# Output product of a fused attention and FFN kernel: the sums and low parts of each chunk from the fifth on moved from GpSimd to VectorE

## The chip, the cores and the metric

One NeuronCore of one Trainium2 chip runs the whole program. The metric is the device time of one execution in microseconds, as the median of three runs. Engines are written as in the profile: PE is TensorE (PEld its weight loads), DVE is VectorE, ACT is ScalarE, POOL is GpSimd, SP is SyncE, which here only issues DMAs.

## The reference

```python
def reference(q, k, v, moe_w1, moe_w2, moe_w3, moe_w_out, moe2_w_in, moe2_w_out):
    attn = attention(q, k, v)            # 4 x 8 heads, 576 positions, causal window of 64, head_dim 64
    x = attn.transpose(0, 2, 1, 3).reshape(2304, 512)
    h = np.maximum(np.maximum(x @ moe_w1, x @ moe_w2), x @ moe_w3)   # 512 -> 768
    x = h @ moe_w_out                                                # 768 -> 512
    h = x @ moe2_w_in                                                # 512 -> 2048
    g = np.where(h >= 1, h, np.where(h <= -1, 0.0, (h + 1) ** 2 / 4))
    return g @ moe2_w_out                                            # 2048 -> 512, the output product
```

## The kernel before

Attention and the first FFN come first, then the product with `moe2_w_in`, and last the output product `g @ moe2_w_out`, which is the only part that the change touches. Each float32 operand is used as two numbers of fewer bits, a high part and a low part (what is left of the value after the high part), and a product takes three passes: high with high, high with low, low with high (`PASSES`).

The output product is written as a Strassen-like scheme with seven products in place of eight. It needs seven blocks for each operand: four quarters and three sums of quarters, one quarter being replaced by a difference. `sums` lists the four additions and subtractions that make them:

```python
        return (
            (x[4], x[2], x[3], ALU.add), (x[2], x[0], x[2], ALU.subtract),
            (x[5], x[4], x[0], ALU.subtract), (x[6], x[1], x[5], ALU.subtract),
        )
```

The 2304 tokens are cut into nine blocks of 256, and the 2048 inner dimensions into four pieces, so that there are 36 chunks (`NCH`), numbered k, with `k % 4` the piece and `k // 4` the token block. The fifth chunk is k = 4. For a chunk, `g_load` brings four quarters from DRAM (`g_scratch` in the profile) into a staging tile `plain`, of which there are three. `g_steps` lists eight steps on it: the four sums (`combine`, line 503 in the profile, L503), then for the first four of the seven blocks a copy to the high part on ACT (`act_copy`, L113, 128x1024) and the low part (`low`, L116, 128x1024), then the same two for the last three blocks (128x768). The high and low parts lie in one of four regions, used in turn (`gc[k % 4]`): two in the tile `side`, two in `arena`. The PE then runs 42 matmuls for the chunk (`d_mm`, L940): two halves r, seven products, three passes. The weights of the product stand in `side`, `arena` and `left`. After every fourth chunk `d_out` (L952 on DVE, one copy on ACT) puts the seven products of a token block together from PSUM, in tiles `evt` and `ut`, and sends the result out.

The order on PE, ACT and DVE is the order in which the steps were put into a list by hand-written times (`put2`, `staged`); `chained` holds these three engines to it. The steps of chunk k stand 2.4 chunks ahead of its matmuls, one after the other, with the parts of `d_out` of the token block before in between. POOL's and SP's order follows the program too. A copy to a region waits until PE is through with the chunk that used it four chunks earlier, and a load waits until the low parts of the chunk that used the staging tile three chunks earlier are made.

In the kernel before, from k = 4 on the second sum (i = 1) is made on POOL, and from k = 5 on the low part of the last three blocks too; the rest is on DVE.

Of the kernel before, what the change touches and what calls it, by code (L numbers as in the profile page):

```python
# [68 lines left out]
def kernel(ctx, tc, q, k, v, w1, w2, w3, wo1, wi2, wo2, out, x2d, td, gd):  # L69
# [12 lines left out]
    nc = tc.nc  # L82
# [378 lines left out]
    RA = {1: 0, 2: 1, 7: 2, 4: 3, 5: 4, 6: 5, 3: 6}  # L461
# [126 lines left out]
    for h in range(2):  # L588
        r = slice(h * BL, h * BL + BL)
# [312 lines left out]
    def quarter(x, q):  # L902
        i, j = divmod(q, 2)
        return x[:, 2 * j:2 * j + 2, i * P:(i + 1) * P] if q < 4 else x[:, q].rearrange("p (r t) -> p r t", r=2)
# [5 lines left out]
    def g_steps(k):  # L910
        c, x = gc[k % 4], plain["g", k]
        steps = [
            (combine, (nc.gpsimd if k == 1 or (k > 3 and i == 1) else nc.vector, [quarter(x, q) for q in range(7)], RA, i))
            for i in range(4)
        ]
        for r in (slice(0, 4), slice(4, 7)):
            hi, lo = (o[:, r] for o in c.hl)
            eng = nc.gpsimd if (k < 1 or k > 4) and r.stop == 7 else nc.vector
            steps += [(act_copy, (hi, x[:, r])), (low, (eng, lo, x[:, r], hi))]
        return steps  # L920

# [54 lines left out]
    for k in range(NCH):  # L976
        if k < 4:
            put2((26.4, 27.2, 30.9, 31.9)[k], g_load, k)
            steps_at(((27.05, 27.06, 27.07, 28.06, 29.01, 29.05, 29.57, 29.58),
                      (28.1, 28.11, 28.12, 28.13, 29.9, 30.05, 30.58, 31.05),  # L980
                      (32.02, 32.03, 32.04, 32.05, 32.31, 32.41, 32.33, 32.43),
                      (32.70, 32.71, 32.72, 32.73, 32.74, 32.76, 32.75, 32.77))[k], g_steps, k)
        else:
            put2(end + CU * (k - 3.4 - (0.4 if k > 4 else 0.0)), g_load, k)
            staged(put2, end + CU * (k - 2.4), 0.06, 8, g_steps, k)
# [30 lines left out]
```

## Time and profile before

| what | value |
|---|---|
| median of three runs | 783.17 us (783.16 to 783.36) |
| profiled execution | 782.92 us |
| its span, first to last instruction | 781.1 us |
| mean granted TensorE clock | 0.987 of full speed |
| busy: PE, DVE, ACT, POOL | 750.4, 511.4, 424.2, 379.8 us |

The busy times are sums over the span, and a busy PE is not PE at its peak: matmuls are pipelined and the ends of the records are modelled, so that how fast PE gets on is better read from the starts of equal pieces of work. The output product fills the last quarter of the span.

### The profile page before, as it was taken

What the parts mean: (1) busy time and instruction counts of PE and PEld (TensorE: products, weight loads), DVE (VectorE), ACT (ScalarE), POOL (GpSimd) and SP (SyncE); (2) the same over time, 40 slices, a digit from 0 to 9 for tenths busy, and PEclk for the clock granted to TensorE, in tenths of its full rate; (3) what the DMA queues carried; (4) which work ended last, traced back from release to release, by engine and by line L of the source; (5) the groups of instructions that cost most, each with busy time, mean ns of one, the idle gap of its engine ahead of it and who ended that gap; (6) DMA issues with size and microseconds to landing.
All of it is one profiled execution on the core that took longest, in us unless ns stands there. A gap on an engine that the chain in (4) does not pass through costs nothing.

```text
span 781.1 us, 17634 instructions
## 1 busy us (share of the span) xinstructions
PE 750.4 (96%) x6824; PEld 728.1 (93%) x6824; DVE 511.4 (65%) x1074; ACT 424.2 (54%) x855; POOL 379.8 (49%) x409
## 2 busy tenths in 40 slices
PE   4798999999999999999999999999999999999997
PEld 3598999999999999999999999999999999999997
DVE  4777334455634454632656687767878899999996
ACT  5897645455464454552448766767685333333332
POOL 1767422544544363553448433731377445555552
PEclk9599999999999999999999999999999999999999
DMA  9999641447767549543445543554556344344341
GB/s 269 264 259 262 162 110 47 144 152 184 227 136 251 202 110 253 197 169 119 135 137 188 200 152 122 178 200 173 195 186 202 123 135 122 122 137 134 113 132 55
DMA packets 158244, 130.00 MB, mean 166 GB/s; under 512 B 94928, under 2 KB 139984, under 8 KB 158160
## 3 DMA queue, kind: packets, MB, share of 16 engines
q1 hardware_dynamic: 135552, 86.13, 39.8%
q10 hardware_dynamic: 19024, 28.06, 9.8%
q0 software_dynamic: 3584, 14.68, 4.8%
q8 instruction: 53, 0.87, 0.5%
q14 instruction: 31, 0.25, 0.1%
HBM read 85.85 MB, written 42.99 MB: 165 GB/s over the span
## 4 chain that ended last, share of the span: by engine, by line
PE 56%; DVE 15%; issue 8%; ACT 7%; POOL 4%; SPq 3%; DMA 3%; ACTq 1%; POOLq 0%; DVEq 0%
PE ps L428 22%; PE ps L450 8%; DVE plain L503 7%; PE cc L747 5%; PE ce L747 5%; PE ca L747 5%; SPq L267 3%; PE cb L747 2%; DVE arena L116 2%; DVE side L116 2%; POOL plain L503 2%; ACT arena L113 2%; PE pps L381 1%; PE sps L339 1%; PE ops L402 1%
## 5 line engine op out<-in xcount | busy, mean ns | idle before, releaser
L428 PE MATMUL ps<-xt,arena 128*128 128x256 f32 x1944 | 237.6, 282 | 6.0 <-ACT xt L113 2.9
L428 PEld LDWEIGHTS ps<-xt,arena 128*128 128x128 f32 x1944 | 231.7, 190 | 8.8 <-ACT xt L113 3.1
L503 DVE TENSOR_TENSOR plain<-plain 128x256 f32<-128x256 f32 (+1 forms) x140 | 128.2, 919 | 3.0 <-DMA plain<-g_scratch 1.3
L116 POOL TENSOR_TENSOR arena<-plain,arena 128x256 fp32r<-128x256 f32 (+2 forms) x70 | 76.8, 1125 | 75.3 <-ACT arena L113 67.2
L437 DVE TENSOR_TENSOR ht<-ps,ht 128x256 f32<-128x256 f32 x108 | 45.3, 420 | 94.8 <-PE ps L428 50.8
L113 ACT ACTIVATE arena<-plain 128x1024 fp32r<-128x1024 f32 (+1 forms) x64 | 61.2, 959 | 66.4 <-POOL plain L503 53.9
L116 POOL TENSOR_TENSOR side<-plain,side 128x768 fp32r<-128x768 f32 (+2 forms) x40 | 56.1, 1422 | 69.8 <-ACT side L113 69.8
L450 PE MATMUL ps<-h,arena 128*128 128x256 f32 x648 | 79.6, 281 | 0.8 <-ACT ht L113 0.8
L450 PEld LDWEIGHTS ps<-h,arena 128*128 128x128 f32 x648 | 76.9, 188 | 2.0 <-issue 1.0
L116 POOL TENSOR_TENSOR h<-ht,h 128x256 fp32r<-128x256 f32 x54 | 44.4, 823 | 68.7 <-ACT h L113 68.4
L113 ACT ACTIVATE side<-plain 128x1024 fp32r<-128x1024 f32 (+3 forms) x48 | 45.4, 965 | 58.2 <-POOL plain L503 44.5
L113 ACT ACTIVATE h<-ht 128x256 fp32r<-128x256 f32 x54 | 22.6, 418 | 81.6 <-DVE ht L437 81.5
L372 POOL TENSOR_TENSOR sm<-sm,rs 128x512 f32<-128x512 f32 (+1 forms) x36 | 35.8, 995 | 59.6 <-DVE rs L371 44.8
L362 ACT ACTIVATE sm<-sm,nm 128x128 f32<-128x128 f32 (+1 forms) x144 | 55.2, 389 | 5.0 <-DVE nm L350 4.2
L210 DVE CUSTOM_DVE_ANT_0 wt<-wst,wt 128x1024 uint16<-128x1024 uint16 (+1 forms) x44 | 45.7, 1046 | 2.4 <-ACT wst L113 1.1
L835 ACT ACTIVATE ut<-ut 128x288 f32<-128x288 f32 x64 | 43.9, 686 | 2.0
L116 DVE TENSOR_TENSOR arena<-plain,arena 128x1024 fp32r<-128x1024 f32 (+3 forms) x28 | 34.8, 1248 | 15.1 <-ACT arena L113 15.1
L503 POOL TENSOR_TENSOR plain<-plain 128x256 f32<-128x256 f32 x36 | 30.8, 855 | 20.5 <-POOL arena L116 6.2
L113 ACT ACTIVATE x2s<-ps 128x256 f32<-128x256 f32 x36 | 13.8, 383 | 49.4 <-PE ps L450 36.4
L116 DVE TENSOR_TENSOR side<-plain,side 128x1024 fp32r<-128x1024 f32 (+3 forms) x25 | 31.0, 1243 | 13.9 <-ACT side L113 13.8
L116 POOL TENSOR_TENSOR arena<-wt,arena 128x512 fp32r<-128x512 f32 x24 | 35.3, 1498 | 9.3 <-ACT arena L113 9.1
L116 DVE TENSOR_TENSOR xt<-ops,xt 128x512 fp32r<-128x512 f32 (+1 forms) x22 | 13.0, 591 | 39.2 <-ACT xt L113 39.2
(144 smaller groups left out, 1622.2 us busy)
## 6 DMA issues: line engine op xcount, KB each, us to landing
g_scratch<-ut ACTq DMA_DIRECT2D x64, 288.0 KB, 2.5
plain<-g_scratch SPq DMA_DIRECT2D x36, 512.0 KB, 3.8
plain<-t_scratch SPq DMA_DIRECT2D x16, 896.0 KB, 4.7
wst<-in_moe_w_out SPq DMA_DIRECT2D x22, 512.0 KB, 4.7
wst<-in_moe_w SPq DMA_DIRECT2D x18, 512.0 KB, 6.5
wst<-in_moe_w_in SPq DMA_DIRECT2D x16, 512.0 KB, 5.0
t_scratch<-wt POOLq DMA_DIRECT2D x16, 512.0 KB, 3.4
vr<-in_v SPq DMA_DIRECT2D x24, 256.0 KB, 4.7
```

The lines of the kernel that those rows point to most:

```text
L113: nc.scalar.activation(dst, src, AF.Copy, scale=scale)
L116: eng.tensor_tensor(dst, a, b, op=ALU.subtract)
L210: nc.vector.tensor_tensor(t[:, x], t[:, x], st[:, x, 0], op=ALU.add)
L267: nc.sync.dma_start(t[32 * a:32 * a + 32, p], src[b1, 2 * p + a // 2, i1 * BL:(i1 + CH) * BL, 32 * (a % 2):32 * (a % 2) + 32] .rearrange(" ...
L362: nc.scalar.activation(sm[:, p, 0:W], sm[:, p, 0:W], AF.Exp, bias=d["nm"][:, p:p + 1], scale=-1.0, accum_out=ss[:, p:p + 1])
L372: nc.gpsimd.tensor_tensor(sm[:, :, 0:W], sm[:, :, 0:W], rs.unsqueeze(2).to_broadcast([P, NP, W]), op=ALU.mult)
L428: nc.tensor.matmul(ps[:, 0:n], w_col((w, f), wl, kt), xt[:, xl, kt, 0:n], start=(x == 0), stop=(x == len(passes) - 1))
L437: nc.vector.tensor_tensor(t[:, 0:n], ps[:, 0:n], part[j, f][:, 0:n], op=ALU.max)
L450: nc.tensor.matmul(ps[:, 0:n], w_col((3, f), wl, dt), hts[j, f][:, xl, 0:n], start=(x == 0), stop=(x == len(passes) - 1))
L503: eng.tensor_tensor(o, a, b, op=op)
L747: nc.tensor.matmul(o, wt.of(m, wl)[:, kt * P:(kt + 1) * P], wx.of(m, xl)[:, kt], start=start and x == 0, stop=x == len(passes) - 1, skip_g ...
L835: nc.scalar.activation(o, o, AF.Square)
```

## The change

Both conditions that send work of the later chunks to GpSimd are taken away. From k = 4 on the second sum, and from k = 5 on the low part of the last three blocks, are issued on VectorE, in the place of the list where they stood. The condition for the first two chunks stays.

```diff
@@ def g_steps(k)
         c, x = gc[k % 4], plain["g", k]
         steps = [
-            (combine, (nc.gpsimd if k == 1 or (k > 3 and i == 1) else nc.vector, [quarter(x, q) for q in range(7)], RA, i))
+            (combine, (nc.gpsimd if k == 1 else nc.vector, [quarter(x, q) for q in range(7)], RA, i))
             for i in range(4)
         ]
         for r in (slice(0, 4), slice(4, 7)):
             hi, lo = (o[:, r] for o in c.hl)
-            eng = nc.gpsimd if (k < 1 or k > 4) and r.stop == 7 else nc.vector
+            eng = nc.gpsimd if k < 1 and r.stop == 7 else nc.vector
             steps += [(act_copy, (hi, x[:, r])), (low, (eng, lo, x[:, r], hi))]
         return steps
```

The order of DVE at chunks 4, 5 and 6, as a difference; `plain` with a number is the staging tile of one chunk (7856 is chunk 4's, 7893 chunk 5's, 7945 chunk 6's), and a low part is written to `side` or `arena`:

```order
-L503 TENSOR_TENSOR plain_7856<-plain_7856 128x256 x3
+L503 TENSOR_TENSOR plain_7856<-plain_7856 128x256
+L503 TENSOR_TENSOR plain_7856<-plain_7856 128x2x128
+L503 TENSOR_TENSOR plain_7856<-plain_7856 128x256 x2
 L116 TENSOR_TENSOR side_5246<-plain_7856,side_5246 128x1024
 L116 TENSOR_TENSOR side_5246<-plain_7856,side_5246 128x768
-L503 TENSOR_TENSOR plain_7893<-plain_7893 128x256 x3
+L503 TENSOR_TENSOR plain_7893<-plain_7893 128x256
+L503 TENSOR_TENSOR plain_7893<-plain_7893 128x2x128
+L503 TENSOR_TENSOR plain_7893<-plain_7893 128x256 x2
 L116 TENSOR_TENSOR side_5246<-plain_7893,side_5246 128x1024
+L116 TENSOR_TENSOR side_5246<-plain_7893,side_5246 128x768
```

The second sum (128x2x128) now stands between the first and the third, and from chunk 5 on the second low part follows the first one. Further on, DVE at chunk 8 (7997 is chunk 7's staging tile, 8050 chunk 8's) has two parts of `d_out` of the first token block between the sums:

```order
 L503 TENSOR_TENSOR plain_8050<-plain_8050 128x256
 L952 SCALAR_TENSOR_TENSOR ut_5818<-dx0_7802,evt_5817 128x256
+L503 TENSOR_TENSOR plain_8050<-plain_8050 128x2x128
 L503 TENSOR_TENSOR plain_8050<-plain_8050 128x256
 L952 SCALAR_TENSOR_TENSOR ut_5818<-dz0_7803,evt_5817 128x2x256
 L503 TENSOR_TENSOR plain_8050<-plain_8050 128x256
 L116 TENSOR_TENSOR side_5246<-plain_8050,side_5246 128x1024
+L116 TENSOR_TENSOR side_5246<-plain_8050,side_5246 128x768
```

Nothing else on DVE changed its place. POOL had these rows in the output product before, of which a piece over chunks 4 to 8 is shown, and has none of them now:

```order
L503 TENSOR_TENSOR plain<-plain 128x2x128 x2
L116 TENSOR_TENSOR side<-plain,side 128x768
L503 TENSOR_TENSOR plain<-plain 128x2x128
L116 TENSOR_TENSOR arena<-plain,arena 128x768
L503 TENSOR_TENSOR plain<-plain 128x2x128
L116 TENSOR_TENSOR arena<-plain,arena 128x768
L503 TENSOR_TENSOR plain<-plain 128x2x128
L116 TENSOR_TENSOR side<-plain,side 128x768
```

In all 32 sums and 31 low parts went from POOL to DVE. The rows of PE, ACT and SP are the same before and after.

## Rows read from the trace of the kernel before

**Rows 1.** The page, parts 1: span, busy time and instructions of each engine.

```profile
span 781.1 us, 17634 instructions
...
PE 750.4 (96%) x6824; PEld 728.1 (93%) x6824; DVE 511.4 (65%) x1074; ACT 424.2 (54%) x855; POOL 379.8 (49%) x409
```

**Rows 2.** PE in order of time, output product: start us, us, what.

```profile
593.74 0.87 PE L940 MATMUL dy<-arena,side 128*128 128x256 f32 x6
...
603.71 0.88 PE L940 MATMUL dy<-left,arena 128*128 128x256 f32 x6
...
608.66 0.88 PE L940 MATMUL dy<-side 128*128 128x256 f32 x6
...
613.64 0.86 PE L940 MATMUL dy<-arena,side 128*128 128x256 f32 x6
...
629.02 0.76 PE L940 MATMUL dy<-side 128*128 128x256 f32 x5
630.16 0.38 PE L940 MATMUL dy<-side 128*128 128x256 f32 x1 [0.38 <-POOL side L116]
...
634.65 0.86 PE L940 MATMUL dy<-arena,side 128*128 128x256 f32 x6
...
771.63 1.58 PE L940 MATMUL dy<-left,arena 128*128 128x256 f32 x12
```

**Rows 3.** Busy time by stretch, output product.

```profile
593.74:613.64 19.90, 19.90 (x171) 19.90 (x170) 17.57 (x19) 7.36 (x9) 11.09 (x10) 1.00 0.50 157
...
634.65:655.76 21.11, 20.58 (x171) 20.03 (x170) 19.31 (x22) 7.68 (x9) 11.06 (x9) 1.00 0.42 124
655.76:771.63 115.87, 113.20 (x926) 110.25 (x925) 105.99 (x118) 42.43 (x50) 60.37 (x45) 1.00 0.39 115
```

**Rows 4.** Waits from 600 us on: who, for whom, us in total, times, longest.

```profile
ACT arena L113 <- POOL plain L503: 53.9, 16, 3.6
...
POOL arena L116 <- ACT arena L113: 35.3, 16, 2.2
...
PE dy L940 <- POOL side L116: 2.4, 7, 0.4
```

**Rows 5.** POOL in order of time, one round of four chunks.

```profile
635.46 0.92 POOL L503 TENSOR_TENSOR plain<-plain 128x256 f32<-128x256 f32 x1 [0.41 <-POOL side L116]
638.56 1.89 POOL L116 TENSOR_TENSOR arena<-plain,arena 128x768 fp32r<-128x768 f32 x1 [2.18 <-ACT arena L113]
640.87 0.74 POOL L503 TENSOR_TENSOR plain<-plain 128x256 f32<-128x256 f32 x1 [0.42 <-POOL arena L116]
...
656.57 0.92 POOL L503 TENSOR_TENSOR plain<-plain 128x256 f32<-128x256 f32 x1 [0.41 <-POOL side L116]
```

**Rows 6.** DVE in order of time: without and beside POOL.

```profile
591.54 1.70 DVE L503 TENSOR_TENSOR plain<-plain 128x256 f32<-128x256 f32 x4 [1.31 <-DMA plain<-g_scratch]
...
601.74 2.08 DVE L116 TENSOR_TENSOR arena<-plain,arena 128x1024 fp32r<-128x1024 f32 x2
...
638.65 2.08 DVE L503 TENSOR_TENSOR plain<-plain 128x256 f32<-128x256 f32 x1
...
642.40 0.41 DVE L503 TENSOR_TENSOR plain<-plain 128x256 f32<-128x256 f32 x1
```

**Rows 7.** DVE groups by form, 613.64 to 771.63 us.

```profile
L503 DVE TENSOR_TENSOR plain<-plain 128x256 f32<-128x256 f32 x90 | 98.4, 1093 | 0.8
...
L952 DVE SCALAR_TENSOR_TENSOR evt<-dx,evt 128x512 f32<-128x512 f32 x8 | 5.4, 678 | 0.0
...
L952 DVE SCALAR_TENSOR_TENSOR evt<-dy,evt 128x256 f32<-128x256 f32 x8 | 3.3, 412 | 0.0
```

**Rows 8.** ACT in order of time: an issue and a copy.

```profile
626.57 0.65 ACTq L965 DMA_DIRECT2D out<-ut  x1
...
636.42 1.06 ACT L113 ACTIVATE arena<-plain 128x1024 fp32r<-128x1024 f32 x1 [3.59 <-POOL plain L503]
```

**Rows 9.** DMA issues, 590 to 640 us: size, us to landing.

```profile
plain<-g_scratch SPq DMA_DIRECT2D x10, 512.0 KB, 3.8
```

## Prediction

> **What bounds the kernel now.** I read the page first. PE is busy for 750.4 of 781.1 us [rows 1], so a change on DVE and POOL can matter only where PE waits. Records of PE end at modelled times, so I read its pace from the starts of chunks (PE in order of time). Chunks 1 to 4 of the output product start PE work at 593.74 and end where chunk 5 begins, at 613.64 [rows 2]: four chunks in 19.90 us, 4.98 each, with PE busy all the time at a granted clock of 1.00 [rows 3]. That is the pace of PE alone. From chunk 5 on it is not held: chunk 9 begins at 634.65 [rows 2], 21.01 us later, and the next round of four takes 21.11 us, still at 1.00 [rows 3]. So the loss is not the clock. Within chunk 8, which starts at 629.02, a matmul waits at 630.16 for a low part from POOL [rows 2]; the list of waits has this seven times for `side` alone [rows 4].
>
> What paces POOL? The waits name a ring: ACT waits 53.9 us for POOL's sums (into `arena`), POOL waits 35.3 us for ACT's copies there [rows 4]. POOL in order of time shows it: sum at 635.46, then 2.18 us idle for ACT, then the low part at 638.56 for 1.89 us, then the next sum at 640.87 [rows 5]. From 635.46 to 656.57 POOL makes four such turns in 21.11 us, exactly PE's round. POOL with ACT in series sets the pace, and PE follows.
>
> DVE looks nearly full at the same time: 19.31 of 21.11 us [rows 3]. But its sums take 1093 ns on average [rows 7], while the same form took 0.41 us at 642.40, when POOL ran nothing, and 2.08 us at 638.65, when POOL had started a low part 0.09 us earlier [rows 5, 6]. The 2.08 us end 0.28 us behind POOL's. Most of DVE's busy time is therefore waiting behind POOL.
>
> **The change part by part.** *POOL.* 32 sums and 31 low parts leave it. The ring ends, and from chunk 4 on nothing runs beside DVE.
>
> *DVE per chunk.* Without POOL four sums took 1.70 us, and the two low parts 2.08 us [rows 6]; both rows hold whole sequences, waits between dependent sums included. That is 3.78 us. Per four chunks: 4 x 3.78 = 15.12, and the five parts of `d_out`, three of 0.41 and two of 0.68 [rows 7], 2.59; together 17.7 us. ACT's first copy needs only the first two sums: it starts at about 0.85, takes 1.06 [rows 8], and with 0.03 us for each hand-over (an estimate; the copy at 636.42 starts 0.04 us behind POOL's sum [rows 5, 8]) ends at 1.97, when DVE has been through the sums for 0.27 us. So a chunk without `d_out` between its sums costs 0.85 + 0.03 + 1.06 + 0.03 + 2.08 = 4.05 us. In two chunks of four a part of 0.41 and one of 0.68 us stand among the sums, the wait vanishes, and the cost is 3.78 + 1.09 = 4.87 us. In one chunk a part of 0.41 us comes first and ACT then issues the output DMA, 0.65 us [rows 8], ahead of its copy, which starts 0.22 us late: 4.05 + 0.41 + 0.22 = 4.68. The round: 4.05 + 2 x 4.87 + 4.68 = 18.5 us on DVE, against 19.90 for PE. DVE is done 1.4 us earlier per round, and PE becomes the bound.
>
> *Start.* DVE has no stock at first. It ends chunk 3's low parts at 601.74 + 2.08 = 603.82 [rows 6]; 4.05 us later, at 607.87, chunk 4 is ready, and PE starts it at 608.66 [rows 2]. Chunk 5 is ready at 611.92, for 613.64; chunk 6 at 615.97, for some 618.6. The lead grows from 0.8 to 1.7 to 2.6 us and then by 1.4 us a round.
>
> *What is late next.* The sums wait for a load: 3.8 us to landing [rows 9], asked for when the low parts three chunks earlier are made. DVE then has two chunks to do, at least 8.1 us, so the load is hidden with 4.3 us to spare. Copies into the regions wait for PE to finish a chunk four back; by then the stock is about three chunks, and DVE merely idles. Parts of `d_out` on DVE wait for PE's products; at this position PE owes them only when DVE is nearly four chunks ahead. Each of these waits would leave PE supplied, so I cost them at nothing; without that cover one would cost what rival 1 costs.
>
> *Sum.* PE goes from chunk 4 at 608.66 to the start of chunk 35, the last, without waiting: 31 chunks, that is seven rounds of 19.90 (139.30) and chunks 32 to 34. Those are a round less its last kind, which took 608.66 - 603.71 = 4.95 us [rows 2]: 14.95 us. Chunk 35 then starts at 608.66 + 154.25 = 762.91 instead of 771.63 [rows 2]. The gain is 8.72 us. The rest, from the start of chunk 35 to the end, 781.1 - 771.63 = 9.47 us, depends on PE and the last `d_out` and stays. The span becomes 772.4 us; the profiled execution's own 782.92 us becomes 774.2, and the median of the runs, 0.25 us above it, 774.4 us.
>
> Bounds of what was not seen: no trace row has a 128x2x128 sum from chunk 4 on running on DVE, though the four sums at 591.54 include one, so 0 to 0.2 us per chunk more; times 4 that takes at most 0.8 of the spare 1.4 us, and costs nothing. PE's free pace rests on one round; chunk 4 alone at 4.98 us and the round's mean agree, so I allow 0.1 us a round each way, 0.8 us in all. No reason appears for PE to get faster than that.
>
> **A rule against it.** The trace shows DVE busy for 91% of a round (19.31 of 21.11) [rows 3], and the change puts 63 more instructions on it. The Trainium skill (Perfetto Trace Analysis, Optimizing Scalar/DVE Operations) says that with a saturated DVE it may make sense to hand some work to other engines, even GPSIMD. By that the change goes the wrong way; rival 2 prices it. The same section warns that the two engines share a read port, so that moving work between them might not help, and SBUF — State Buffer (SBUF: two separate sides) calls it an exclusive lock, held for a whole instruction, between a DVE operation with two SBUF inputs and a GpSimd operation. The 2.08 us beside POOL and the 0.41 us alone agree with the lock [rows 6]. By the lock the sum above stands; by the first rule read alone it would be rival 2's.
>
> **The rivals.** *1. DVE becomes the bound.* DVE's 18.5 us leave only 7% of a round. If each of the 29 instructions of a round is followed by 0.07 us more than I counted (2.0 us), or a wait for ACT falls on every chunk, DVE needs about 20.5 us, and PE follows it: 7.75 rounds x 0.6 = 4.7 us of the gain are lost, 779 us. It decides from 19.90 us on. Against it: my durations are taken from rows with their gaps, and neighbouring records even overlap by some 0.07 us.
>
> *2. Sums stay slow.* If sums take 1.09 us whatever POOL does, a round is 16 x 1.09 + 4 x 2.08 + 2.59 = 28.4 us on DVE; PE follows, 7.75 x (28.4 - 21.1) = 57 us more, 840 us. It is slower than now from 21.1 us a round, which is a mean sum of (21.1 - 10.9) / 16 = 0.64 us. For it: the mean [rows 7]. Against it: 0.41 and 1.70 us for four [rows 6].
>
> *3. Nothing changes.* PE's lost 1.2 us a round could come from elsewhere (a copy on ACT, a load), and the releaser be misnamed: 783 us. Against it: POOL's turn equals PE's round to 0.01 us [rows 3, 5].
>
> **How the numbers follow.** My forecast has 0.84, with 773.6 to 775.4 us of its own; rival 1 has 0.09 (775.4 to 781), rival 2 has 0.04, rival 3 has 0.03. The likeliest time is 774.4 us. The range 773.4 to 777.4 us takes in the forecast with the bounds of PE's pace and the nearer half of rival 1. About 0.2% (1.6 us) is what a measurement can tell from no change: faster has 0.84 + 0.09 = 0.93, same 0.03, slower 0.04.
>
> **What would show it.** Right: POOL has no records after about 601 us; DVE's 128x256 sums at 0.41 to 0.48 us; starts of PE's chunks four apart 19.9 us apart up to the last; no wait of PE for a low part; DVE's busy share near 85%, with idle time behind ACT or PE. Wrong: sums above 0.64 us, a round of PE above 20 us with waits for DVE (rival 1 or 2), or an unchanged 21.1 us (rival 3). The forecast also fails if chunk 4 or 5 starts late, which would show a missing lead in the start.

## Result and the profile after

The changed kernel takes 773.54 us (median of four runs, 773.28 to 775.8) against 783.26 us for the kernel before (four runs, 783.16 to 783.4): a ratio of 0.9882, with a 95% interval of 0.9863 to 0.9901. Forecast were 774.4 us and a range of 773.4 to 777.4 us. The profiled execution took 773.50 us, with a span of 771.7 us.

The page of the changed kernel, part 1, answers to [rows 1]:

```profile
span 771.7 us, 17563 instructions
...
PE 745.5 (97%) x6824; PEld 727.3 (94%) x6824; DVE 490.1 (64%) x1137; ACT 424.7 (55%) x855; POOL 292.8 (38%) x346
```

DVE has 63 more instructions and is busy for 21 us less; POOL has 63 fewer and is busy for 87 us less. PE in order of time, at the starts of chunks 4, 8, 12 and 35, answers to [rows 2]:

```profile
608.04 0.88 PE L940 MATMUL dy<-side 128*128 128x256 f32 x6
...
627.93 0.88 PE L940 MATMUL dy<-side 128*128 128x256 f32 x6
...
647.82 0.88 PE L940 MATMUL dy<-side 128*128 128x256 f32 x6
...
762.23 1.58 PE L940 MATMUL dy<-left,arena 128*128 128x256 f32 x12
```

A round of four chunks takes 19.89 us from chunk 4 on. From chunk 4 to chunk 35 PE needs 762.23 - 608.04 = 154.19 us; the forecast had 154.25. The busy time by stretch over the same rounds answers to [rows 3]:

```profile
608.04:627.93 19.89, 19.89 (x170) 19.89 (x169) 18.06 (x33) 9.47 (x11) 0.00 (x0) 1.00 0.51 151
627.93:647.82 19.89, 19.89 (x170) 19.89 (x169) 18.53 (x35) 7.92 (x10) 0.00 (x0) 1.00 0.49 144
647.82:762.23 114.41, 114.41 (x968) 114.41 (x967) 89.89 (x159) 42.64 (x50) 0.00 (x0) 1.00 0.40 120
```

PE never pauses, POOL has nothing, and DVE falls from 18.53 of 19.89 us in the second round to 89.89 of 114.41 us (79%) later, when it has run as far ahead as it may. The waits from 600 us on, which answer to [rows 4], show the same thing:

```profile
ACT side L113 <- DVE plain L503: 37.9, 22, 2.4
ACT arena L113 <- DVE plain L503: 32.4, 14, 4.9
...
DVE arena L116 <- ACT arena L113: 12.5, 12, 2.1
DVE evt L952 <- ACT evt L113: 10.8, 1, 10.8
ACT arena L113 <- PE dw L940: 9.9, 4, 2.5
```

No row has PE waiting for anyone. ACT waits for PE to release regions, and DVE has finished its last low part 10.8 us before it must put the last token block together. DVE in order of time, from the first sum of chunk 10 to that of chunk 14, answers to [rows 6]:

```profile
628.95 1.68 DVE L503 TENSOR_TENSOR plain<-plain 128x256 f32<-128x256 f32 x4
631.09 2.09 DVE L116 TENSOR_TENSOR arena<-plain,arena 128x1024 fp32r<-128x1024 f32 x2 [0.47 <-ACT arena L113]
633.10 0.42 DVE L503 TENSOR_TENSOR plain<-plain 128x256 f32<-128x256 f32 x1
633.43 0.42 DVE L952 SCALAR_TENSOR_TENSOR evt<-dy,evt 128x256 f32<-128x256 f32 x1
633.77 0.75 DVE L503 TENSOR_TENSOR plain<-plain 128x256 f32<-128x256 f32 x2
634.43 0.69 DVE L952 SCALAR_TENSOR_TENSOR evt<-dx,evt 128x512 f32<-128x512 f32 x1
635.03 0.42 DVE L503 TENSOR_TENSOR plain<-plain 128x256 f32<-128x256 f32 x1
...
637.46 0.42 DVE L503 TENSOR_TENSOR plain<-plain 128x256 f32<-128x256 f32 x1
...
641.91 0.42 DVE L503 TENSOR_TENSOR plain<-plain 128x256 f32<-128x256 f32 x1
...
646.52 1.67 DVE L503 TENSOR_TENSOR plain<-plain 128x256 f32<-128x256 f32 x4
```

The four chunks cost DVE 4.15, 4.36, 4.45 and 4.61 us, together 17.57 us for a round, which leaves 2.3 us of PE's 19.89. The sums as a group (613.64 to 762 us) answer to [rows 7]: 419 ns in place of 1093.

```profile
L503 DVE TENSOR_TENSOR plain<-plain 128x256 f32<-128x256 f32 x116 | 46.2, 419 | 0.7
```

The span fell by 9.4 us. Of that, 162.97 - 154.19 = 8.78 us lie between the starts of chunks 4 and 35. The rest, from chunk 35 to the end, takes 771.7 - 762.23 = 9.47 us, as before. The remaining 0.62 us were there when chunk 4 started (608.66 before, 608.04 after), and the code up to there is the same. They do not come from one place. The same matmuls of the first FFN begin at 46.71 us in the kernel before and at 46.00 in the changed one; at 305.9 us the two are 0.03 us apart; and shortly before 311.00 the kernel before waits 0.71 us for ACT, where the changed one runs on. PE in order of time, before:

```profile
305.92 4.36 PE L428 MATMUL ps<-xt,arena 128*128 128x256 f32 x36
311.00 4.24 PE L428 MATMUL ps<-xt,arena 128*128 128x256 f32 x34 [0.71 <-ACT ht L113]
```

PE in order of time, changed:

```profile
305.89 9.35 PE L428 MATMUL ps<-xt,arena 128*128 128x256 f32 x78
```

In the traces below chunk 4 starts between 606.80 and 608.22 us, so this part differs from run to run.

### The profile page after: what moved, and what is told of

Its sections match the earlier page's. It is cut to its first block, busy times and chain, and to the rows that moved or that the text cites. A ratio compares the mean times of both kernels' runs of the same rounds, so it can differ in the third digit from the quotient of the medians.

```text
span 771.7 us, 17563 instructions
## 1 busy us (share of the span) xinstructions
PE 745.5 (97%) x6824; PEld 727.3 (94%) x6824; DVE 490.1 (64%) x1137; ACT 424.7 (55%) x855; POOL 292.8 (38%) x346
## 3 DMA queue, kind: packets, MB, share of 16 engines
HBM read 85.85 MB, written 42.99 MB: 167 GB/s over the span
## 4 chain that ended last, share of the span: by engine, by line
PE 82%; ACT 5%; issue 4%; DVE 2%; POOL 2%; ACTq 0%; DVEq 0%; POOLq 0%
PE ps L428 25%; PE ps L450 10%; PE dz L940 7%; PE dy L940 7%; PE dx L940 7%; PE cc L747 6%; PE ce L747 5%; PE ca L747 5%; PE dw L940 3%; PE cb L747 3%; PE ops L402 2%; PE sps L339 2%; PE pps L381 2%; POOL arena L116 1%; ACT sm L362 1%
## 5 line engine op out<-in xcount | busy, mean ns | idle before, releaser
L503 DVE TENSOR_TENSOR plain<-plain 128x256 f32<-128x256 f32 (+1 forms) x172 | 77.8, 470 | 2.9 <-DMA plain<-g_scratch 1.2
L116 DVE TENSOR_TENSOR arena<-plain,arena 128x1024 fp32r<-128x1024 f32 (+3 forms) x44 | 49.1, 1143 | 21.5 <-ACT arena L113 21.5
L116 POOL TENSOR_TENSOR arena<-plain,arena 128x256 fp32r<-128x256 f32 (+1 forms) x54 | 47.0, 906 | 40.9 <-ACT arena L113 32.8
L116 DVE TENSOR_TENSOR side<-plain,side 128x1024 fp32r<-128x1024 f32 (+3 forms) x40 | 44.7, 1137 | 11.8 <-ACT side L113 11.6
L116 POOL TENSOR_TENSOR side<-plain,side 128x288 fp32r<-128x288 f32 (+2 forms) x25 | 25.7, 1059 | 36.5 <-ACT side L113 36.5
L844 DVE SCALAR_TENSOR_TENSOR ut<-ut,evt 128x864 f32<-128x864 f32 x32 | 36.2, 1130 | 1.6 <-ACT ut L835 1.6
```

What stands on the lines that cost most here:

```text
L116: eng.tensor_tensor(dst, a, b, op=ALU.subtract)
L503: eng.tensor_tensor(o, a, b, op=op)
L844: nc.vector.scalar_tensor_tensor(o, o, 2.0 ** WS, x, op0=ALU.min, op1=ALU.max)
```

## Experiments

Two theories stood for PE's lost 1.2 us per round. A: POOL and DVE keep each other from SBUF, so the work on POOL slows DVE, and all of it has to go. B: the ring in POOL's order (its sum, ACT's copy, its low part, its next sum) sets the pace, and cutting the ring is enough. All kernels compute the same output. Each ratio below is against the kernel before, timed beside that experiment (medians 782.46 to 783.53 us). In the cuts of the edits, `...` stands for lines left out.

### 1. Only the sum moved (e1), only the low part moved (e2)

Both edits are against the changed kernel.

```diff
 # e1
+            eng = nc.gpsimd if (k < 1 or k > 4) and r.stop == 7 else nc.vector
 # e2
+            (combine, (nc.gpsimd if k == 1 or (k > 3 and i == 1) else nc.vector, [quarter(x, q) for q in range(7)], RA, i))
```

> One half of the change alone: the second sum of chunks 4 to 35 goes to DVE, the low part of the last three blocks (chunks 5 to 35) stays on POOL. Theory A (POOL and DVE lock each other out, and the ring sum on POOL, copy on ACT, low part on POOL only adds to it): the first sum of each chunk still takes about 2.05 us behind POOL's low part, so DVE needs 4.7 + 2 x 5.4 + 5.35 = 20.9 us per four chunks, more than PE's 19.9, and the time is about 7.75 x 1.0 = 7 us above the changed kernel, some 780 us (778 to 783). Theory B (only the ring counts, and slow sums are a side show): the ring is cut, PE runs at 19.9 us per four chunks, and the time is that of the changed kernel, 773.5 us.

> The other half alone: the low part of the last three blocks goes to DVE, the second sum stays on POOL. Theory A: the sum on POOL takes 0.74 to 0.92 us and holds up one sum of DVE, so a chunk costs DVE 4.55 us without parts of the final sum, 4.9 us with two of them and 5.1 us with one, 19.4 us per four chunks, just under PE's 19.9: the time is that of the changed kernel within 2 us, 773.5 to 775.5 us. Theory B: the ring is cut here too, 773.5 us. A rival C (any sum on POOL is late for ACT, and so for PE): the time stays near 780 us.

Measured: 774.38 us (ratio 0.988, 0.9865 to 0.9895) and 774.02 us (0.9879, 0.9858 to 0.9901). Each half alone gives the whole gain, and in both traces PE waits for nobody in the output product. e2 is as both theories had it, and rival C, with its 780 us, falls. For e1 theory A's number was too high, though its mechanism is in the trace. DVE in order of time in e1:

```profile
635.07 2.07 DVE L503 TENSOR_TENSOR plain<-plain 128x256 f32<-128x256 f32 x1
...
645.35 0.42 DVE L503 TENSOR_TENSOR plain<-plain 128x256 f32<-128x256 f32 x1
645.69 0.42 DVE L952 SCALAR_TENSOR_TENSOR ut<-dw,evt 128x256 f32<-128x256 f32 x1
646.02 2.53 DVE L503 TENSOR_TENSOR plain<-plain 128x256 f32<-128x256 f32 x3
...
650.16 3.32 DVE L503 TENSOR_TENSOR plain<-plain 128x256 f32<-128x256 f32 x4
...
655.10 2.08 DVE L503 TENSOR_TENSOR plain<-plain 128x256 f32<-128x256 f32 x1
```

In three chunks of four the first sum still takes 2.07 us behind POOL's low part, and DVE has almost no pause, but its round is 655.10 - 635.07 = 20.03 us and not 20.9. Most of the difference is the chunk with one part of `d_out`: it takes 650.16 - 645.35 = 4.81 us and not 5.35. POOL's low part starts there only at 645.49, so the first sum gets ahead of it, the part of `d_out` runs beside it, and only the second sum is held. The two chunks with two parts took 5.14 us each in place of 5.4, and the one without a part 4.94 in place of 4.7. The round is PE's own pace within 0.15 us. So e1 doesn't tell A from B.

### 2. All work left on POOL, only its order turned (e5)

```diff
 ...
-            staged(put2, end + CU * (k - 2.4), 0.06, 8, g_steps, k)
+            staged(put2, end + CU * (k - 2.4), 0.06, 7 + (k < 5), g_steps, k)
+            if k > 4:
+                put2(end + CU * (k - 1.4) + 0.09, lambda k=k: (lambda s: s[0](*s[1]))(g_steps(k)[7]))
 ...
```

This is applied to the kernel before; `chained` also holds POOL to the list's order in these chunks.

> The kernel before, with all its work on POOL, but POOL's order turned: the low part of a chunk comes behind the second sum of the next chunk, so that ACT never waits for a sum that stands behind POOL's own low part. If the ring (sum on POOL, copy on ACT, low part on POOL, next sum) set the pace before, cutting it is enough: DVE then needs about 0.34 + 0.85 + 2.0 + 1.14 = 4.35 us for a chunk, 19.9 us per four with the parts of the final sum, PE's own pace, and the time is 773.5 to 777 us. If instead the amount of work on POOL beside DVE (the lock) set the pace, nothing is saved, since that amount is unchanged: 783 us.

Measured: 775.79 us (0.9908, 0.9893 to 0.9923). POOL in order of time: a low part follows the sum of the next chunk at once, where it waited 2.18 us for ACT before [rows 5].

```profile
643.29 0.74 POOL L503 TENSOR_TENSOR plain<-plain 128x256 f32<-128x256 f32 x1 [1.89 <-DVE plain L503]
643.99 2.04 POOL L116 TENSOR_TENSOR side<-plain,side 128x768 fp32r<-128x768 f32 x1
```

The busy time from 655.8 to 739 us shows PE full with POOL busy for 60% of the stretch; POOL was not less loaded before (42.99 of the same 83.20 us):

```profile
655.80:739.00 83.20, 83.20 (x705) 83.20 (x704) 77.20 (x95) 34.71 (x40) 49.81 (x36) 1.00 0.49 146
```

The 2 us by which it stays behind the changed kernel lie mostly in one wait at chunk 5, whose low part now stands behind a sum of chunk 6 (PE in order of time):

```profile
614.22 0.39 PE L941 MATMUL dy<-arena,side 128*128 128x256 f32 x1 [1.23 <-POOL side L116]
```

With the same instructions on every engine PE is free of waits after that. The order on POOL was the cause of the lost time in the kernel before, as B has it.

But A's hold, DVE kept waiting behind POOL's low part, is a link of that ring. POOL's sum overwrites a quarter that DVE's first sum of the same chunk reads, so it has to wait for that one. In e5 the profile names this wait, in the rows of POOL above: DVE's first sum ends at 642.74 + 0.41 = 643.15, and POOL's sum starts 0.14 us later, at 643.29. DVE in order of time in e5:

```profile
642.74 0.41 DVE L503 TENSOR_TENSOR plain<-plain 128x256 f32<-128x256 f32 x1
```

In the kernel before, the 0.41 and 0.42 us ahead of POOL's sums are put down to POOL's own low part, which had been done for as long [rows 5]. What ended them was DVE's first sum, held behind that low part: it ends at 638.65 + 2.08 = 640.73, and POOL's sum starts 0.14 us later, at 640.87 [rows 5, 6]. In one turn of the four DVE's first sum gets ahead of the low part, and POOL then goes on without a wait. POOL in order of time, before:

```profile
649.32 1.91 POOL L116 TENSOR_TENSOR side<-plain,side 128x768 fp32r<-128x768 f32 x1 [2.48 <-ACT side L113]
651.19 0.92 POOL L503 TENSOR_TENSOR plain<-plain 128x256 f32<-128x256 f32 x1
```

DVE in order of time beside it:

```profile
649.10 0.42 DVE L503 TENSOR_TENSOR plain<-plain 128x256 f32<-128x256 f32 x1
```

The three other waits make 1.25 us of the 21.11 us round, as much as PE lost. Without them the ring would take 19.86 us, PE's own pace (an estimate from these rows). e1, e2 and e5 each cut the ring with the hold in it; no run takes the hold alone out, so how the loss divides between the two is not shown.

### 3. POOL's low part a second time, for nobody (e3)

```diff
 ...
+        if k > 4:
+            steps.append((low, (nc.gpsimd, spare, x[:, 4:7], c.hl[0][:, 4:7])))
 ...
```

> The changed kernel, and POOL in addition computes the low part of the last three blocks of chunks 5 to 35 a second time into a spare piece of a tile that nobody reads; PE, ACT and DVE keep their instructions. Theory A (lock): the first sum of each chunk on DVE again takes about 2 us in place of 0.42, DVE needs about 17.6 + 4 x 1.6 = 24 us per four chunks, PE follows, and the time is 7.75 x 4 = 32 us above the changed kernel, some 805 us (790 to 810). Theory B (only the ring counts): POOL's work feeds nobody, so the time stays at 773.5 us, at most 1 us more.

Measured: 805.80 us (1.0284, 1.0268 to 1.03), theory A's number. POOL's result goes nowhere, but DVE is held up. DVE in order of time:

```profile
633.70 3.72 DVE L116 TENSOR_TENSOR side<-plain,side 128x1024 fp32r<-128x1024 f32 x2 [0.71 <-ACT side L113]
```

The pair of low parts takes 3.72 us where it took 2.09 in the changed kernel: POOL's low part (634.55 to 636.61) got in between the two, so the delay mostly falls on the second low part and not, as expected, on the next sum. The pair ends at 637.42, and PE, which needs it, goes on at 637.47. PE in order of time:

```profile
634.86 0.76 PE L943 MATMUL dy<-arena,side 128*128 128x256 f32 x5
637.47 0.38 PE L943 MATMUL dy<-arena,side 128*128 128x256 f32 x1 [1.86 <-DVE side L116]
```

So A's mechanism exists too, and costs 32 us where DVE holds all the work. In the kernel before it did not set the pace by filling DVE, as A has it, but only as the link of the ring shown under e5.

### 4. How much DVE could still take (e4, e6, e8)

```diff
 ...
+        if k > 4:
+            steps += steps[3:4] * 2        # e4: the last sum two more times; e6: once
+            steps.append((sub, (nc.vector, spare, x[:, 0], x[:, 1])))    # e8
 ...
```

> The changed kernel, and on DVE each of chunks 5 to 35 makes its last sum two more times, after its low parts (the same values into the same place). In the changed kernel's trace DVE's round of four chunks takes 17.6 us where it is not held (615.40 to 633.10 and on to 650.68 us less), against 19.9 for PE. Eight more sums of 0.33 to 0.42 us make 20.3 to 21.0 us. If DVE's spare time is as read (2.3 us per round), PE follows DVE now and the time is 7.75 x (20.3 to 21.0 less 19.9) = 3 to 8.5 us above the changed kernel, 776.5 to 782 us. If DVE has more spare time than that, 773.5 us; if DVE was already the bound in the changed kernel, 7.75 x 2.7 to 3.4 = 21 to 26 us more, 795 to 800 us.

> The changed kernel with one more sum per chunk on DVE from chunk 5 on (the last sum once more, after the low parts). Two more cost 21.25 - 17.6 = 3.65 us per four chunks, so one costs about 1.85, and DVE needs 19.45 us, still under PE's 19.9: no change, 773.5 us (to 774.5). If DVE has no such reserve: some 7 us more.

> The changed kernel, and on DVE one more 128x256 subtraction per chunk from chunk 5 on, behind the low parts, of two of the first four blocks into a spare piece of a tile that nobody reads, so that it waits for nobody and nobody for it. At 0.34 to 0.42 us DVE's round of four chunks grows from 17.6 to some 19.1 us, under PE's 19.9: no change, 773.0 to 774.5 us.

Measured: 783.53 us for e4 (1.0005, 0.9993 to 1.0016), 773.00 us for e6 (0.9873, 0.9854 to 0.9892), 773.62 us for e8 (0.9885, 0.9867 to 0.9903). DVE in order of time in e4, at the same part of `d_out` one round apart:

```profile
639.32 0.42 DVE L954 SCALAR_TENSOR_TENSOR evt<-dy,evt 128x256 f32<-128x256 f32 x1
...
660.57 0.42 DVE L954 SCALAR_TENSOR_TENSOR evt<-dy,evt 128x256 f32<-128x256 f32 x1
```

The round is 21.25 us. A repeated sum costs (21.25 - 17.57) / 8 = 0.46 us, while the extra subtraction of e8, which needs nothing from the instruction before it, is followed after 0.33 us (629.99 to 630.32); so the repeated sum waits for the one before it, and the loss came out 1.5 us above the upper end expected. One extra instruction per chunk is free (4 x 0.46 = 1.85 us per round), two are not (3.7 us). So the point from which DVE bounds the changed kernel lies between these two, as its trace has it with 2.3 us, and rival 1 was that close.

### 5. The same extra work where only the sum was moved (e7, e9)

These are e1 with the extra instruction of e6 (e7) and of e8 (e9).

> The same extra sum in the kernel in which only the second sum was moved (low parts on POOL). Its DVE needed 20.03 us per four chunks without a pause, so it stood at PE's pace with no reserve although its time equals the changed kernel's. With 1.85 us more it needs 21.9 us, PE follows, and the time is about 7.75 x 2.0 = 15 us above the changed kernel less the 1 to 2 us of stock at the start, 786 to 789 us. If the first sums' 2.07 us are a wait that an extra sum can fill, the time stays near 774 us.

Measured: 795.10 us (1.0149, 1.0131 to 1.0167), more than expected, and not for the reason tested. The repeated sum writes a block that POOL's low part still reads, so DVE waits for POOL by a dependence. DVE in order of time:

```profile
645.45 0.76 DVE L503 TENSOR_TENSOR plain<-plain 128x256 f32<-128x256 f32 x2 [1.73 <-POOL arena L116]
```

> The same extra subtraction in the kernel in which only the second sum was moved. In it DVE needed 20.03 us per four chunks. If the time in which DVE is locked out behind POOL's low part cannot be used by DVE for another instruction that reads two tiles in SBUF, a round grows to 21.4 us, PE follows, and the time is 7.75 x 1.5 = 11.6 us above, less 1 to 2 us of stock at the start: 783 to 786 us. If the extra subtraction fits into the 1.65 us in which the first sum stood behind POOL, that is, if the first sum waited for something else, the time stays at 774 us.

e9 has no such dependence: 789.09 us (1.0087, 1.0066 to 1.0108), above the range expected by 3 us. DVE in order of time:

```profile
642.18 2.07 DVE L116 TENSOR_TENSOR side<-plain 128x256 fp32r<-128x256 f32 x1
644.18 0.41 DVE L503 TENSOR_TENSOR plain<-plain 128x256 f32<-128x256 f32 x1
```

Now the extra subtraction takes the 2.07 us, and the sum behind it 0.41. The delay belongs to whichever instruction with two inputs in SBUF stands behind POOL's low part, and the extra one adds its own time. PE's chunks 12 and 16 begin 21.93 us apart:

```profile
648.49 0.75 PE L943 MATMUL dy<-side 128*128 128x256 f32 x5
...
670.42 0.75 PE L943 MATMUL dy<-side 128*128 128x256 f32 x5
```

That is 0.5 us more than 20.03 + 4 x 0.34. The chunk with one part of `d_out` accounts for it: it takes 653.38 - 647.67 = 5.71 us where e1 took 4.81, while the three others grew by 0.34 us each. POOL's low part starts at 647.80, now ahead of the first sum, so this sum is held, and the part of `d_out`, which ran beside the low part in e1, comes behind it. DVE in order of time in e9:

```profile
647.67 0.42 DVE L116 TENSOR_TENSOR side<-plain 128x256 fp32r<-128x256 f32 x1
648.00 2.06 DVE L503 TENSOR_TENSOR plain<-plain 128x256 f32<-128x256 f32 x1
649.98 0.41 DVE L955 SCALAR_TENSOR_TENSOR ut<-dw,evt 128x256 f32<-128x256 f32 x1
```

The comparison stands: the same instruction costs e1 15 us and the changed kernel nothing. Moving both halves gains no more time than moving one, but it leaves DVE the largest reserve: its round is 17.57 us against PE's 19.89, where e1 has 20.03, e2 19.06 (634.95 to 654.01) and e5 18.34 (638.12 to 656.46). e2 and e5 were not given extra work, so what they could take is not shown.

## Why the prediction was right

**The bound before.** POOL with ACT in series paced PE: e5 keeps every instruction and cuts only that series, and PE runs at its own pace. It holds, with a link that I left out: DVE's first sum, held behind POOL's low part, stands in that series and makes 1.25 us of its 21.11. And it is not so that most of DVE's busy time was waiting behind POOL: the twelve sums of a round were longer by 12 x (1.09 - 0.42) = 8.0 us, of 19.31.

**DVE per chunk.** Sums of 0.42 us without POOL and 2.09 us for a pair of low parts came as taken from the rows. The round was put at 18.5 us and is 17.57. The term that was off is the chunk with two parts of `d_out`, 4.87 forecast and 4.36 and 4.45 measured. About half of that is overlap: I added whole records, and neighbours overlap by about 0.08 us (a record of 0.42 us is followed 0.33 to 0.34 us later). The other half is waits that I counted although they vanish: the four sums in a row, 1.68 us, hold two waits of a sum for the one before it, which then follows it after 0.46 us; where a part of `d_out` stands between the two, as in chunk 11, no such wait is left. A chunk without `d_out` came out at 4.15, forecast 4.05. The spare time was thus 2.3 us, not 1.4, and rival 1, though e4 shows it to be real, was further off than stated. The time did not hang on this term, since PE was the bound with either value.

**The start.** Chunk 4 was to be ready 0.8 us ahead of PE. Its low parts end at 605.16 + 2.10 = 607.26 us in the changed trace's DVE rows, and PE starts it at 608.04: 0.78 us.

**The sum.** 8.72 us forecast, 8.78 measured between chunks 4 and 35. The other 0.6 us of the span lie ahead of chunk 4, where the code is the same, and the median lies 0.04 us above the profiled execution, not 0.25. Neither follows from the change. They put the time 0.9 us below the likeliest one and 0.14 us above the lower end of the range; that it stayed inside is luck.

**The rivals.** Rival 2 (sums slow whatever POOL does) falls with the 419 ns, rival 3 with PE's rounds. The rule against the change, to hand work to other engines when DVE is saturated (the Trainium skill, Perfetto Trace Analysis, Optimizing Scalar/DVE Operations), would have misled here: of the 19.31 us behind DVE's 91%, 8.0 us were sums held behind POOL, and with 63 more instructions its busy time fell by 21 us. The Trainium skill's warning in the same section about the shared port, and the exclusive lock in the Trainium skill, SBUF — State Buffer (SBUF: two separate sides), agree with e3 (a pair of low parts 3.72 us in place of 2.09) and e9 (a subtraction 2.07 us in place of 0.42).

**What the prediction did not say.** It treated the two moves as one remedy. Either of them alone takes the whole gain, and a turn of two instructions on POOL takes 7.0 of the 9.7 us.

## What to carry to other kernels

When an engine off the bound paces it, look for the series in its order (its result, another engine's answer, its next step) before its load: e5 took back 7 us by moving an instruction past one other. Name every link of it: a wait that is put down to an engine that had long been done belongs to another one, here DVE. Read an engine's fullness from what the same instruction takes when the neighbour is idle (0.42 us against 1.09 here), not from its busy share. Two versions of equal time can differ in reserve; one extra instruction per chunk showed which of them stands at the edge.

## What the runs showed of the hardware

What POOL holds up on DVE depends on where the operands lie, in the rows below. POOL in order of time in e5:

```profile
653.08 2.04 POOL L116 TENSOR_TENSOR arena<-plain,arena 128x768 fp32r<-128x768 f32 x1
```

DVE in order of time beside it:

```profile
653.32 0.68 DVE L953 SCALAR_TENSOR_TENSOR evt<-dx,evt 128x512 f32<-128x512 f32 x1
653.92 1.48 DVE L503 TENSOR_TENSOR plain<-plain 128x256 f32<-128x256 f32 x1
```

The first reads PSUM and one tile in SBUF and takes 0.68 us, as it does with POOL idle; the next reads two blocks in SBUF and ends only at 655.40, 0.28 us behind POOL's end at 655.12. The same 0.28 us stood in the kernel before [rows 5, 6]. The two differ in operation too, but that is not what decides: in the kernel before, a TENSOR_TENSOR with one operand in PSUM (`ce`) runs beside POOL in 0.45 us, as it does with POOL idle (0.46 us at 574.93). DVE in order of time, before:

```profile
577.00 0.45 DVE L820 TENSOR_TENSOR evt<-ce,evt 128x288 f32<-128x288 f32 x1
```

POOL in order of time beside it:

```profile
575.62 2.45 POOL L116 TENSOR_TENSOR side<-plain,side 128x768 fp32r<-128x768 f32 x1 [3.89 <-ACT side L113]
```
